# Key products of chunks 24 to 31 made four to fifteen steps earlier, from compact inputs, and copied out by ScalarE

## The chip, the cores and the metric

One core of a Trainium2 chip. The metric is the device time of one execution in microseconds. Three runs of the kernel before gave 883.72, 884.16 and 885.75 us; the median, 884.16 us, is what the changed kernel is compared with.

## The reference

Three layers follow each other. The first, linear attention with a delta rule, is the one that the change touches. With 4 batches, 8 heads, 768 tokens and heads of 48 numbers it does, for each head, token by token:

```python
k_n = k / (np.linalg.norm(k, axis=-1, keepdims=True) + 1e-06)
for t in range(S):
    y[:, :, t] = np.einsum('bhd,bhde->bhe', q[:, :, t], state)
    v_old = np.einsum('bhde,bhd->bhe', state, kt)
    state = state + bt[:, :, :, None] * np.einsum('bhd,bhe->bhde', kt, vt - v_old)
```

The second layer adds the real part of a 2D Fourier transform to its input, normalises and applies a two-layer network (384 to 1536 to 384). The third is a gated network with a 768 by 768 matrix over the tokens. Both come after attention and are not touched.

## The kernel before

**Chunks and steps.** Attention is worked in chunks of 64 tokens: 4 batches of 12 chunks, 48 chunks in all, of 8 heads each (4 pairs of heads, two heads side by side on the partitions). The batches are staggered by four chunks, and the list `SEQ` gives the order. A loop over steps `t` from -3 to 47 (line 516) is a software pipeline: in step t chunk t is finished, and later chunks are prepared. What is recorded in one step stands ahead of what is recorded in the next on each engine (`chain`, line 75), and each engine works through its own list in order.

**What is done for a chunk.** `stage_a` (line 211) multiplies the chunk's keys with its queries and keys on TensorE into a PSUM bank of the tag X (4 banks) and copies the products, masked, into a buffer `gak` that holds four chunks. `solve` (line 267) takes eight chunks at a time, a block: on VectorE it inverts 32 x 32 triangles in some 200 small operations; the class `Spread` deals them out over eight steps, and the block after it is collected by `prep` (line 248) near the end of the same solve. `merge` joins the triangles (TensorE L378 and L380, ScalarE L382 and L385, `diag` L366). `values` scales the values by the norms (ScalarE L402, or VectorE L399 late in the loop). `stage_b` (TensorE L409, ScalarE L414) makes `WU`, `stage_c` (TensorE L425, VectorE L426) makes `cw`, and `stage_d` (TensorE L438 and L440, ScalarE L451 and L455) writes the output and the next state. The order of a step is values, mask, part of the solve, stage_d of chunk t, stage_c of t+1, part of the solve, stage_a, merge and stage_b of t+2, the rest of the step's share of the solve.

**Two ways to make the key products.** Chunks 0 to 7 are made by their own code ahead of the loop. For chunks 8 up to `HEAD` (24 before) `stage_a` reads a compact input `kc` (two chunks per 448 KB transfer), makes eight matmuls of 48 rows (L219) and has ScalarE copy the bank out in three operations (L194, L195, L225), with no mask but for one quarter. What the copy leaves out is made good later: by `mask_q` on VectorE (one operation of 512 columns, L241, or two of 256, L245) in the even step two before the chunk is used, and by five memsets on GpSimd in `root` (L145). All sixteen chunks of this kind are made ahead of the loop, while VectorE solves block 0. From chunk `HEAD` on `stage_a` reads `kq` (one chunk per 448 KB), makes four matmuls of 112 rows (L221) and has VectorE mask and copy in a single operation (L227). These are made in step t for chunk t + 20 (`R`), so chunks 24 to 31 in steps 4 to 11. `prep` of block 3 waits, in the recording, until chunk 31 has been made (line 321).

**Buffers and queues.** `gak` buffers of chunks 0 to 11, 24 to 35 come from the pool `pe`, three of them, the others from another pool. The key inputs have five buffers, refilled by `load_kq` through SyncE's queue: up to step 1 the loop starts the loads of chunks `HEAD` to `HEAD` + 4, and `stage_a` starts the rest.

Of the kernel before, what the change touches and what calls it, by code (L numbers as in the profile page):

```python
# [7 lines left out]
F32 = mybir.dt.float32  # L8
# [14 lines left out]
HP = H // 2  # L23
# [4 lines left out]
GA = C + 2 * D  # L28
NT = B * S // 128

HEAD = 24

TOK = np.concatenate([np.arange(S // 2), [S // 2], S - np.arange(1, S // 2)])

# [31 lines left out]
class Kernel:  # L66
# [51 lines left out]
    def attention(self, cp, pg, pe, p, x, filler, after_solves):  # L118
# [17 lines left out]
        def root(blk):  # L136

            Tf, T, Tw, sq = preps[blk]
            n0 = pe.tile([128, 32], F32, name="n0", bufs=2)
            nc.scalar.sqrt(n0, sq)  # L140
            if blk in (1, 2):

                for n in (16, 8, 4, 2, 1):
                    t = Tw[:, n : n + 1056].rearrange("p (m q) -> p m q", q=66 * n)[:, :, : 32 * n]
                    nc.gpsimd.memset(t.rearrange("p m (r w) -> p m r w", w=32)[:, :, :, :n], 0.0)  # L145
            preps[blk] = Tf, T, sq, n0
# [22 lines left out]

        def ring(bc):  # L170

            gak = (pe if bc // 4 % 6 < 3 else p).tile([128, 4, HP, GA], F32, name="gak", bufs=3)
            for i in range(4):
                gas[bc + i] = gak[:, i]
            gas[bc, 4] = gak
# [16 lines left out]
        def copy_g(out, in_):  # L192

            nc.scalar.activation(out[:, :, 32:], in_[:, :, 32:], AF.Copy, scale=mk[:, 4 * C : 4 * C + 1])  # L194
            nc.scalar.copy(out=out[:, :, :32], in_=in_[:, :, :32])  # L195

        def mask_a(bc, n):
            m = 2 * C if SEQ[bc][1] < HALF else 0
            return mk[:, m : m + n].unsqueeze(1)

        def load_kq(bc):
            if bc < HEAD:
                if 8 <= bc and bc % 2 == 0:
                    t = pe.tile([112, HP, 4 * C], F32, name="kq", bufs=CF["kq"]).rearrange("p a n -> p (a n)")
                    kqs[bc], kqs[bc + 1] = (t[:, i * HP * 2 * C : (i + 1) * HP * 2 * C].rearrange("p (a n) -> p a n", a=HP) for i in range(2))
                    load(out=t.rearrange("p (c n) -> p c n", c=2), in_=a["kc"][:, bc - 8 : bc - 6])
            elif bc < NBC:
                kqs[bc] = pe.tile([112, HP, 4 * C], F32, name="kq", bufs=CF["kq"])
                load(out=kqs[bc], in_=a["kq"][bc])

        def stage_a(bc):
            kq = kqs.pop(bc)
            if bc % 4 == 0:
                ring(bc)
            pa = self.bank("pa", [128, HP, 2 * C])
            for hp in range(HP):
                if bc < HEAD:
                    for r, q in ROWS:
                        nc.tensor.matmul(pa[q, hp], lhsT=kq[r, hp, C:], rhs=kq[r, hp], start=True, stop=True)  # L219
                else:  # L220
                    nc.tensor.matmul(pa[:, hp], lhsT=kq[:, hp, 2 * C :], rhs=kq[:, hp, : 2 * C], start=True, stop=True)  # L221
            if bc < HEAD:

                copy_g(gas[bc][:, :, C : 2 * C], pa[:, :, C:])
                nc.scalar.copy(out=gas[bc][:, :, :C], in_=pa[:, :, :C])  # L225
            else:
                nc.vector.tensor_tensor(  # L227
                    out=gas[bc][:, :, : 2 * C], in0=pa, in1=mask_a(bc, 2 * C).to_broadcast([128, HP, 2 * C]), op=MUL
                )
            if bc < HEAD:  # L230
                if bc % 2 and bc + 2 * CF["kq"] < HEAD:
                    load_kq(bc + 2 * CF["kq"] - 1)
            else:
                load_kq(bc + CF["kq"])
            seen_a[0] = bc + 1
# [152 lines left out]
        def load_kv(bc):  # L388
            load(out=gas[bc][:, :, C:], in_=a["kv"][bc])
# [70 lines left out]
        for n in "kq":  # L460
            t = p.tile([128, 4, HP, GA], F32, name="gak", bufs=3).rearrange("p a b c -> p (a b c)")[:112, :2048]
# [38 lines left out]
        Spread(solve(0), 0).finish()  # L500
        for i in range(4):
            nc.scalar.copy(out=both0(i, 0), in_=pairs0("q", i))
        for bc in range(8, HEAD):
            stage_a(bc)
        busy(CF["last"], 512)
        mask_q(0)
# [8 lines left out]
        T0 = -3  # L515
        for t in range(T0, NBC):
            j, i = divmod(t + 11, 8)
            if i == 0 and j < NB:
                if solver:
                    solver.finish()  # L520
                solver = Spread(solve(j), 25100 if j < NB - 1 else 26500)
            part = (lambda f: solver.upto((i + f) / 8)) if j < NB else (lambda f: None)
            if light(t) and solver:
                solver.finish()
                solver = None

            if 0 <= t + 2 < NBC and (not light(t) or (t + 2) % 8 == 0):
                values(t + 2)
            if t % 2 == 0 and 2 <= t + 2 < HEAD:
                mask_q(t + 2)  # L530
            part(c1)
            if t >= 0:
                stage_d(t)
                if SEQ[t][1] == NC - 1:
                    fill.extend(filler(SEQ[t][0]))
            new = t % 8 == 5 and t + 3 < NBC
            if new:

                merge((t + 3) // 2, True, False)
                load_kv(t + 3)  # L540
                load_kv(t + 4)
                diag((t + 3) // 2)
            if 0 <= t + 1 < NBC:
                stage_c(t + 1)
            if light(t + 1) and t + 3 < NBC and (t + 3) % 8:
                values(t + 3)
            part(c2)
            if HEAD <= t + R < NBC:
                stage_a(t + R)
            if t < T0 + CF["kq"]:  # L550
                load_kq(HEAD + t - T0)
            odd = t % 2 and (t + 3) // 2 < NBC // 2
            if t == NBC - 12:
                solver.finish()
                loads, tail = after_solves()
            if t % 2 == 0 and t % 8 != 4 and t + 4 < NBC:
                diag((t + 4) // 2)
            if (odd or light(t + 1)) and 0 <= t + 2 < NBC:
                stage_b(t + 2)
            if odd:  # L560
                g = (t + 3) // 2
                merge(g + 1, (g + 1) % 4 > 0, True)
                if (t + 5) % 8 and t + 5 < NBC:
                    load_kv(t + 5)
                    load_kv(t + 6)
            if light(t + 1):

                for _ in range(CF["dfs"][t - (NBC - 12)]):
                    while fill and next(fill[0], 1) == 1:
                        fill.pop(0)  # L570
                for _ in range(CF["cvt"][t - (NBC - 12)]):
                    next(tail, None)
            elif not odd and 0 <= t + 2 < NBC:
                stage_b(t + 2)
            if 2 <= t + 4 < NBC:
                load_qt(t + 4)
            part(1)
            self.chain()
            next(loads, None)
            self.chain()  # L580
# [647 lines left out]
```

## Time and profile before

| what | value |
|---|---|
| three runs | 883.72, 884.16, 885.75 us |
| the profiled execution: its own time | 881.6 us |
| span of its instructions | 879.8 us |
| mean granted TensorE clock | 0.986 of full speed |
| TensorE busy | 845.1 us, 7219 instructions |
| VectorE busy | 577.6 us, 1790 instructions |
| ScalarE busy | 392.8 us, 970 instructions |
| GpSimd busy | 72.5 us, 85 instructions |

The attention loop runs from 42 us to 290 us of the span; the two networks fill the rest. In the rows PE is TensorE, PEld its weight load, DVE VectorE, ACT ScalarE, POOL GpSimd and SP SyncE. Each fp32 matmul of the kernel leaves two records (384 records of L438 for 192 matmuls), and records of matmuls overlap, so that a stretch in which TensorE is 100% busy can hold small stalls. The median of the three runs lies 2.56 us above the profiled execution's own time.

### The profile page before, as it was taken

Reading aid. Unit: us, or ns where it says so; the run is one execution under the profiler, and the core shown is the slowest. Engines: PE = TensorE matmul, PEld = TensorE weight load, DVE = VectorE, ACT = ScalarE, POOL = GpSimd, SP = SyncE. Lnnn points to the kernel's source line nnn. Section 1 sums busy time; section 2 is a strip of 40 time slices with the busy share of each in tenths; the row PEclk is TensorE's granted clock in tenths of the full one; section 3 lists DMA queues with packets and bytes.
Section 4 is the critical chain, followed back from the end, with each engine's and each line's share of the span. In section 5 each row is a group of like instructions: output and inputs, shape, how many; then the busy total and the mean of one; then the engine's idle time right before and its main releaser. Section 6 shows DMA issues by size and latency. Waiting matters only on the chain.

```text
span 879.8 us, 18531 instructions
## 1 busy us (share of the span) xinstructions
PE 845.1 (96%) x7219; PEld 816.1 (93%) x7219; DVE 577.6 (66%) x1790; ACT 392.8 (45%) x970; POOL 72.5 (8%) x85
## 2 busy tenths in 40 slices
PE   7879999999998999999999999999999999999998
PEld 7769989998987898999999999999899899899998
DVE  5999999998868897784654993331566552552622
ACT  1569888888765534222122342221352341431511
POOL 2000000000000000000000000000123232231321
PEclk8969999999999999999999999999999999999999
DMA  8265665523461800001022410101122210000001
GB/s 219 66 185 138 169 183 159 158 83 103 127 178 38 322 1 2 1 1 28 1 70 76 129 28 24 48 7 45 58 74 69 71 28 28 27 1 28 28 1 54
DMA packets 57673, 67.21 MB, mean 76 GB/s; under 512 B 31825, under 2 KB 48946, under 8 KB 57586
## 3 DMA queue, kind: packets, MB, share of 16 engines
q1 hardware_dynamic: 57586, 66.03, 26.0%
q8 instruction: 57, 0.93, 0.4%
q14 instruction: 30, 0.25, 0.1%
HBM read 53.62 MB, written 4.72 MB: 66 GB/s over the span
## 4 chain that ended last, share of the span: by engine, by line
PE 78%; DVE 16%; DMA 2%; ACT 2%; issue 1%; POOL 0%; ACTq 0%; SPq 0%; DVEq 0%; POOLq 0%
PE bankX L812 15%; PE bankY L828 14%; PE bankX L951 11%; PE bankY L971 6%; PE bankX L937 5%; PE bankX L912 5%; PE bankY L438 3%; PE bankY L440 3%; PE bankY L425 3%; PE bankY L409 3%; PE bankX L221 2%; DVE tm L308 2%; DVE Ts L313 2%; PE bankX L631 2%; PE bankZ L380 2%; PE bankV L828 1%
## 5 line engine op out<-in xcount | busy, mean ns | idle before, releaser
L812 PE MATMUL bankX<-uh,w 128*128 128x384 f32 x504 | 136.1, 337 | 0.7 <-DVE ul L740 0.7
L828 PE MATMUL bankY<-w,hh 128*128 128x384 f32 x504 | 117.1, 338 | 1.2 <-DVE w L714 1.2
L820 DVE SCALAR_TENSOR_TENSOR hl<-bankX,hh 128x384 fp32r<-128x384 f32 x84 | 46.5, 553 | 97.8 <-ACT hh L819 97.8
L819 ACT ACTIVATE hh<-bankX 128x384 fp32r<-128x384 f32 x84 | 41.2, 491 | 153.7 <-PE bankX L812 150.9
L951 PE MATMUL bankX<-ws,vh 128*128 128x384 f32 x384 | 97.6, 336 | 0.0
L812 PEld LDWEIGHTS bankX<-uh,w 128*128 128x128 f32 x504 | 91.6, 188 | 1.2 <-DVE ul L740 0.9
L828 PEld LDWEIGHTS bankY<-w,hh 128*128 128x128 f32 x504 | 89.9, 188 | 2.3 <-DVE w L714 2.0
L812 PE MATMUL bankX<-ul,w 128*128 128x384 f32 x252 | 84.5, 335 | 0.0
L929 POOL TENSOR_TENSOR vl<-v,vh 128x512 fp32r<-128x512 f32 x24 | 31.8, 1334 | 510.4 <-DMA x<-un 433.9
L438 PE MATMUL bankY<-WU,gak 128*112 128x96 f32 (+1 forms) x384 | 69.6, 269 | 2.7 <-ACT x L455 2.7
L828 PE MATMUL bankY<-w,hl 128*128 128x384 f32 x252 | 71.9, 336 | 0.0
L951 PEld LDWEIGHTS bankX<-ws,vh 128*128 128x128 f32 x384 | 69.4, 188 | 0.0
L440 PE MATMUL bankY<-Sb,cw 112*112 112x96 f32 (+1 forms) x352 | 63.8, 263 | 5.5 <-DVE cw L426 4.6
L959 DVE TENSOR_TENSOR g<-bankX,bsb 128x384 f32<-128x384 f32 x32 | 17.7, 556 | 77.9 <-PE bankX L951 72.0
L951 PE MATMUL bankX<-ws,vl 128*128 128x384 f32 x192 | 63.7, 336 | 0.0
L313 DVE TENSOR_TENSOR Ts<-Ts,tm 128x110 f32<-128x110 f32 (+26 forms) x264 | 59.8, 266 | 0.9
L308 DVE TENSOR_TENSOR tm<-Ts 128x110 f32<-128x110 f32 (+26 forms) x264 | 59.4, 265 | 0.4
L438 PEld LDWEIGHTS bankY<-WU,gak 128*112 128x112 f32 (+1 forms) x384 | 51.7, 176 | 6.0 <-ACT x L455 3.4
L409 PE MATMUL bankY<-gak,TT 128*128 128x96 f32 x384 | 52.2, 281 | 3.9 <-ACT gak L402 3.5
L440 PEld LDWEIGHTS bankY<-Sb,cw 112*112 112x112 f32 (+1 forms) x352 | 47.7, 174 | 7.2 <-DVE cw L426 5.7
L414 ACT COPY WU<-bankY 64x384 f32<-64x384 f32 x96 | 45.4, 473 | 18.8 <-PE bankY L409 17.4
L409 PEld LDWEIGHTS bankY<-gak,TT 128*128 128x128 f32 x384 | 48.8, 199 | 4.5 <-ACT gak L402 4.0
(181 smaller groups left out, 1825.9 us busy)
## 6 DMA issues: line engine op xcount, KB each, us to landing
kq<-in_kq_dram SPq DMA_DIRECT2D x24, 448.0 KB, 4.2
qt<-in_qt_dram SPq DMA_DIRECT2D x48, 196.0 KB, 3.7
gak<-in_kv_dram SPq DMA_DIRECT2D x48, 192.0 KB, 3.8
w<-in_w_dram SPq DMA_DIRECT2D x24, 384.0 KB, 7.7
x<-un SPq DMA_DIRECT2D x128, 36.0 KB, 1.9
out_dram<-ot SPq DMA_DIRECT2D x24, 192.0 KB, 2.0
kq<-in_kc_dram SPq DMA_DIRECT2D x8, 448.0 KB, 11.8
s<-in_wi_dram SPq DMA_DIRECT2D x6, 512.0 KB, 4.3
```

What stands on the lines that cost most here:

```text
L308: nc.vector.tensor_tensor(out=tm, in0=T[:, r, k : k + 1].to_broadcast(sh), in1=T[:, k : k + 1, :k].to_broadcast(sh), op=MUL)
L313: nc.vector.tensor_add(o, o, tm)
L409: nc.tensor.matmul(pb[:, hp].rearrange("p t d -> p (t d)"), lhsT=tt[:, o + hp], rhs=kv[:, hp], start=True, stop=True)
L414: nc.scalar.copy(out=o_, in_=pb[hs])
L438: nc.tensor.matmul(pd[:m, hp], lhsT=ak[:, hp, :m], rhs=u[:, hp], start=True, stop=(c == 0))
L440: nc.tensor.matmul(pd[:m, hp], lhsT=cw[:, hp, :m], rhs=sb[:, hp], start=False, stop=True)
L812: nc.tensor.matmul(ph, lhsT=w1[f][i][:, c * 128 : c * 128 + 128], rhs=cur[k][:, c], start=(c + j == 0), stop=(c == 2 and j == 2))
L820: nc.vector.scalar_tensor_tensor(out=hl, in0=ph, scalar=0.0, in1=hh.bitcast(F32), op0=MAX, op1=SUB)
L828: nc.tensor.matmul(acc[t], lhsT=hx[i][:, t * 128 : t * 128 + 128], rhs=w2[e][k], start=(e == 0 and j == 0), stop=(e == 11 and j == 2),)
L912: nc.tensor.matmul(pv, lhsT=xT[t // 3][i][:, c, (t % 3) * 128 : (t % 3) * 128 + 128], rhs=wi[2 * c + 1][k], start=(c + j == 0), stop=(c == ...
L951: nc.tensor.matmul(pv, lhsT=vn[i][:, s, f * 128 : f * 128 + 128], rhs=ws[2 * s + hf][k], start=(s + j == 0), stop=(s == 5 and j == 2),)
L971: nc.tensor.matmul(po, lhsT=gt[i][:, f, t * 128 : t * 128 + 128], rhs=wo[f][k], start=(f + j == 0), stop=(f == 3 and j == 2),)
```

## The change

`HEAD` goes from 24 to 32, so that chunks 24 to 31 are of the compact kind too: they are read from `kc`, made by the eight small matmuls, copied by ScalarE, masked by `mask_q` on VectorE in steps 22 to 28 and by GpSimd in `root` of block 3. They are not made ahead of the loop with the sixteen others but in steps -3, -2, -1 and 0, two in each. No key products are made in steps 4 to 11; from step 12 on everything stands as before. The pool `pe` holds five `gak` buffers in place of three.

```diff
-HEAD = 24
+HEAD = 32
...
-            if blk in (1, 2):
+            if 0 < 8 * blk < HEAD:
...
-            gak = (pe if bc // 4 % 6 < 3 else p).tile([128, 4, HP, GA], F32, name="gak", bufs=3)
+            gak = (pe if bc // 4 % 6 < 3 else p).tile([128, 4, HP, GA], F32, name="gak", bufs=5 if bc // 4 % 6 < 3 else 3)
...
-        for bc in range(8, HEAD):
+        for bc in range(8, HEAD - 8):
             stage_a(bc)
...
             part(c2)
+            if t < T0 + 4:
+                for i in range(2):
+                    stage_a(HEAD - 8 + 2 * (t - T0) + i)
             if HEAD <= t + R < NBC:
                 stage_a(t + R)
```

On ScalarE, at the start of step -2, the list of before reads as follows; `ZS` and `TT` belong to the merge, `gak` in L402 is the values, `WU` the copy of stage_b, and the numbers tell the buffers apart.

```order
L382 ACTIVATE ZS_80<-bankZ 96x8x32
L366 COPY TT_85<-Tc 32x8x32 x2
L382 ACTIVATE ZS_81<-bankZ 96x8x32
L385 COPY TT_85<-bankZ 32x8x64 x2
L402 ACTIVATE gak<-gak,n_all 128x48 x4
L366 COPY TT_86<-Tc 32x8x32 x2
L414 COPY WU_87<-bankY 64x4x2x48 x2
```

In the changed kernel the stretch from the same L366 to the first L402 stands so:

```order
L366 COPY TT_85<-Tc 32x8x32 x2
L194 ACTIVATE gak<-bankX,mk 128x4x32
L195 COPY gak<-bankX 128x4x32
L225 COPY gak<-bankX 128x4x64
L194 ACTIVATE gak<-bankX,mk 128x4x32
L195 COPY gak<-bankX 128x4x32
L225 COPY gak<-bankX 128x4x64
L382 ACTIVATE ZS_81<-bankZ 96x8x32
L385 COPY TT_85<-bankZ 32x8x64 x2
L402 ACTIVATE gak<-gak,n_all 128x48 x4
```

Six copies, those of chunks 24 and 25, have come between the merge's copies; six more stand in each of steps -2, -1 and 0, behind L402, behind L402 and behind L455.

On VectorE, at the end of the solve of block 2 (steps 11 and 12), the list of before reads as follows; L254 and L261 are `prep` of block 3, L327 turns the finished triangles of block 2.

```order
L426 TENSOR_TENSOR cw<-qt,bankY 112x448
L227 TENSOR_TENSOR gak<-bankX,mk 128x4x128
L254 SCALAR_TENSOR_TENSOR Cc<-gak,mk 128x512 x2
L261 STREAM_TRANSPOSE Ts<-Cc 128x1024
L263 COPY sq<-Ts 128x32
L245 TENSOR_TENSOR gak<-gak,mk 128x4x64 x2
L327 STREAM_TRANSPOSE Tc<-Ts 128x16x32 x2
```

In the changed kernel the same place reads:

```order
L254 SCALAR_TENSOR_TENSOR Cc<-gak,mk 128x512 x2
L261 STREAM_TRANSPOSE Ts<-Cc 128x1024
L263 COPY sq<-Ts 128x32
L426 TENSOR_TENSOR cw<-qt,bankY 112x448
L245 TENSOR_TENSOR gak<-gak,mk 128x4x64 x2
L327 STREAM_TRANSPOSE Tc<-Ts 128x16x32 x2
```

The L227 of chunk 31 is gone, and the collecting of block 3 now stands ahead of step 11's `cw` and no longer behind it.

On TensorE, in step 4, before:

```order
L440 MATMUL bankY<-Sb_89,cw 112x96
L221 MATMUL bankX<-kq 128x128 x4
L409 MATMUL bankY<-gak,TT_86 128x96 x4
L438 MATMUL bankY<-WU_88,gak 112x96 x4
L378 MATMUL bankZ<-Tc,gak 32x32 x16
```

And in the changed kernel:

```order
L440 MATMUL bankY<-Sb_89,cw 112x96
L409 MATMUL bankY<-gak,TT_86 128x96 x4
L438 MATMUL bankY<-WU_88,gak 112x96 x4
L378 MATMUL bankZ<-Tc,gak 32x32 x16
L425 MATMUL bankY<-gak,WU_87 112x112 x4
```

The four matmuls of the key products have left step 4, and likewise steps 5 to 11; sixteen of L219 stand in each of steps -3 to 0.

## Rows read from the trace of the kernel before

**Rows 1.** Windows at steps: length; PE, PEld, DVE, ACT, POOL busy; clock; DMA share, GB/s
```profile
42.00:57.76 15.76, 8.37 (x176) 7.44 (x176) 15.11 (x69) 7.55 (x21) 0.83 (x6) 0.58 0.57 152
57.76:75.18 17.42, 16.94 (x218) 16.24 (x217) 16.97 (x69) 16.55 (x46) 0.00 (x0) 0.89 0.56 157
75.18:114.31 39.13, 38.61 (x572) 37.15 (x568) 37.30 (x152) 33.97 (x95) 0.83 (x6) 1.00 0.59 164
...
193.97:230.35 36.38, 33.62 (x524) 31.64 (x520) 33.00 (x94) 30.35 (x78) 0.15 (x1) 1.00 0.32 84
```

**Rows 2.** Chain of waits, 75.18 to 114.31: by line; a piece (start, us)
```profile
by line: PE bankX L221 18.6%; PE bankY L409 17.7%; PE bankY L438 16.9%; PE bankY L425 15.4%; PE bankY L440 15.2%; PE bankZ L380 8.4%; DVE Ts L261 5.1%; PE bankZ L378 3.5%; PE bankY L444 1.9%; DVE cw L426 1.6%; issue 0.3%; DVE sq L263 0.1%
...
77.75 0.92 PE bankX L221 x8
```

**Rows 3.** Groups by line, 76 to 114 us: count, busy us, mean ns, idle before
```profile
L227 DVE TENSOR_TENSOR gak<-bankX,mk 128x512 f32<-128x512 f32 x8 | 5.5, 691 | 0.4 <-PE bankX L221 0.3
```

**Rows 4.** Timeline of ScalarE, steps -3 to -1: start, us, operation, [idle before]
```profile
45.93 0.23 ACT L140 ACTIVATE n<-sq 128x32 f32<-128x32 f32 x1 [8.13 <-DVE sq L263]
...
48.49 0.38 ACT L382 ACTIVATE ZS<-bankZ 96x256 f32<-96x256 f32 x1 [1.21 <-PE bankZ L380]
...
52.58 0.96 ACT L414 COPY WU<-bankY 64x384 f32<-64x384 f32 x2 [0.65 <-PE bankY L409]
...
56.06 0.96 ACT L414 COPY WU<-bankY 64x384 f32<-64x384 f32 x2 [1.49 <-PE bankY L409]
57.98 0.38 ACT L382 ACTIVATE ZS<-bankZ 96x256 f32<-96x256 f32 x1 [0.95 <-PE bankZ L380]
58.37 1.17 ACT L385 COPY TT<-bankZ 32x512 f32<-32x512 f32 x2
```

**Rows 5.** Timeline of ScalarE ahead of the loop: the three copies of one chunk
```profile
36.13 0.37 ACT L194 ACTIVATE gak<-bankX,mk 128x128 f32<-128x128 f32 x1
36.40 0.26 ACT L195 COPY gak<-bankX 128x128 f32<-128x128 f32 x1
36.54 0.39 ACT L225 COPY gak<-bankX 128x256 f32<-128x256 f32 x1
```

**Rows 6.** Windows of L219 alone: PE and PEld busy us (records), clock, DMA
```profile
21.44:23.14 1.70, 1.70 (x16) 1.70 (x18) 0.50 0.00 0
28.02:29.72 1.70, 1.70 (x36) 1.70 (x34) 1.00 0.84 241
```

**Rows 7.** Windows of steps -3 to 1, four us each, as in rows 1
```profile
42.00:46.00 4.00, 0.61 (x32) 0.49 (x32) 3.83 (x5) 0.07 (x1) 0.04 (x1) 0.83 0.56 126
...
54.00:58.00 4.00, 4.00 (x73) 3.66 (x74) 4.00 (x24) 1.54 (x6) 0.00 (x0) 0.50 0.29 78
...
62.00:66.00 4.00, 4.00 (x75) 3.91 (x76) 4.00 (x21) 3.83 (x12) 0.00 (x0) 1.00 0.68 221
```

**Rows 8.** Timeline of VectorE, steps 11 and 12
```profile
112.54 0.69 DVE L227 TENSOR_TENSOR gak<-bankX,mk 128x512 f32<-128x512 f32 x1 [0.28 <-PE bankX L221]
113.15 1.40 DVE L254 SCALAR_TENSOR_TENSOR Cc<-gak,mk 128x512 f32<-128x512 f32 x2
...
116.69 0.76 DVE L245 TENSOR_TENSOR gak<-gak,mk 128x256 f32<-128x256 f32 x2
```

**Rows 9.** Timeline of TensorE: L409 in step -2, the stalls of steps 4 and 13
```profile
50.47 2.02 PE L409 MATMUL bankY<-gak,TT 128*128 128x96 f32 x8 [2.05 <-ACT gak L402]
...
76.14 0.44 PE L440 MATMUL bankY<-Sb,cw 112*112 112x96 f32 x2 [0.52 <-DVE cw L426]
...
119.93 0.43 PE L440 MATMUL bankY<-Sb,cw 112*112 112x96 f32 x2 [1.03 <-DVE cw L426]
```

**Rows 10.** Timeline of VectorE, a mask in step 0, and steps 27 and 28
```profile
58.51 0.69 DVE L241 TENSOR_TENSOR gak<-gak,mk 128x512 f32<-128x512 f32 x1
...
191.30 0.62 DVE L426 TENSOR_TENSOR cw<-qt,bankY 112x448 f32<-112x448 f32 x1 [1.40 <-PE bankY L425]
```

**Rows 11.** Windows around the start of the loop: DMA in the last columns
```profile
36.00:42.00 6.00, 4.68 (x31) 2.25 (x29) 5.93 (x25) 1.65 (x7) 0.00 (x0) 1.00 0.00 0
```

## What the change was predicted to do

> **What bounds the kernel now.** I read three views in this order. First the windows, cut where a step's first matmul of stage_d starts [rows 1]. The third row is the stretch that the change empties, steps 4 to 11: 39.13 us, in which TensorE is busy 38.61 us, VectorE 37.30 and ScalarE 33.97. So two engines are full there and the third nearly. The row above it, steps 0 to 3, already has no key products on TensorE or VectorE; it takes 17.42 us with 16.94, 16.97 and 16.55 us busy, all three full. The first row, steps -3 to -1, is VectorE's: 15.11 of 15.76 us, while TensorE is busy for 8.37 and ScalarE for 7.55. Second the chain of waits of steps 4 to 11 [rows 2]: nearly all of it is TensorE, and the key products, L221, are its largest line with 18.6%. So what leaves TensorE there leaves the path, until the next engine is late. Third the timeline of ScalarE in steps -3 to -1 [rows 4], because it gets the work: its idle time between 47 and 58 us stands in four waits of 1.21, 0.65, 1.49 and 0.95 us, 4.30 us in all. The wait of 8.13 us before them can't be used: the operation that waits is queued ahead of all that is added.
>
> **What leaves steps 4 to 11.** Eight times four matmuls of L221 at 0.92 us [rows 2] are 7.4 us of TensorE, and eight L227 on VectorE [rows 3] at 0.61 us from start to start (112.54 to 113.15 [rows 8]; their durations of 0.69 overlap) are 4.9 us. That would leave 38.61 - 7.4 = 31.2 us on TensorE, 37.30 - 4.9 = 32.4 on VectorE and an unchanged 33.97 on ScalarE [rows 1]. ScalarE becomes the fullest engine, and 33.97 us is the floor of these steps: at best 5.2 us are won, not 7.4. An engine doesn't reach its floor when it hands work back and forth with two others. The nearest rows that show how close it comes are steps 0 to 3, with the same work by kind and ScalarE full: 17.42 / 4 = 4.36 us a step, 34.8 us for eight; the one extra of steps 4 to 11 is L444, 1.9% of the chain or 0.7 us [rows 2], of which I take 0.5. That gives 35.3 us, a gain of 3.8. The other end is steps 28 to 35, which also make no key products and take 36.38 us with each engine busy for under 34 [rows 1]: a gain of 2.75. I take 3.8, as the work of steps 0 to 3 is the nearer (in steps 28 to 35 part of the scaling of the values stands on VectorE), and keep 2.75 and 5.2 as ends.
>
> **What steps -3 to 0 get.** Per chunk TensorE gets sixteen records of L219 and ScalarE three copies. The copies start 0.27 and 0.14 us apart and the last takes 0.39 [rows 5], so a chunk costs 0.80 us by its end, less the some 0.1 us by which an operation overlaps the one behind it; I take 0.75 (ends 0.70 and 1.02, the sum of the durations). Six chunks in steps -3 to -1 are 4.5 us against 4.30 us of idle time [rows 4]: ScalarE leaves these steps 0.2 us late. The waits can be filled only if what they wait for comes in time. Their releasers are TensorE's merge and L409, behind which the new matmuls are queued. At the full clock two chunks take 2 x 16 / 36 x 1.70 = 1.5 to 1.75 us [rows 6] and stand in TensorE's idle time (7.4 of 15.76 us), so they cost nothing; the cover goes if the clock is low, which is the first rival. Step 0 gives two more chunks, 1.5 us, to a ScalarE that has no idle time left: 1.7 us late. Behind these copies are queued diag, then L414 of chunk 2, on which TensorE's L425 and then VectorE's `cw` wait, so the delay reaches all three engines. Steps 1 to 3 have 17.42 - 16.55 = 0.87 us of idle ScalarE time, of which I let it win back 0.5. Step 4 starts 1.2 us late. Ends: 0, if VectorE alone set the pace of these steps, and 4.6, the first rival's.
>
> **Masks, prep and loads.** `mask_q` for chunks 24 to 31 adds two pairs of L245 (0.76 us each [rows 8]) and two L241 (0.69 [rows 10]) to VectorE in steps 22, 24, 26 and 28, 2.9 us. Up to step 26 VectorE has them done before step 27, where it sits idle for 1.40 us [rows 10] and so is not the last; the fourth stands behind that wait, between the collecting of block 5 and the turning of block 4, where VectorE is late, and costs its 0.6. I take 0.6; ends 0 and 2.9. The collecting of block 3 no longer waits for chunk 31: before, it starts at 113.15, behind chunk 31's L227, and step 13 then stalls TensorE for 1.03 us, where step 4, in which the same collecting stands ahead of `cw`, stalls it for 0.52 [rows 9]. I take a gain of 0.5; ends 0 and 1.0. The five memsets on GpSimd stand a step ahead of their first reader and cost nothing. Loads: four more compact transfers, 1.8 MB, go out before the loop where the DMA engines move nothing for 6 us [rows 11], which at 241 GB/s [rows 6] is 7.5 us, some of it before 36 us; eight of 448 KB leave steps 4 to 11. SyncE's queue has passed them before the loop's first loads, which stand behind them. No cost. Chunks 32 on find buffers free earlier than before, with five in place of three.
>
> **Sum.** +1.2 (start), -3.8 (steps 4 to 11), -0.5 (step 13), +0.6 (masks) = -2.5 us. Nothing behind step 28 is changed in order, and the networks start when attention ends, so it is carried to the end. The profiled execution took 881.6 us (1.8 of it around the span), so its like takes 879.1; it lies 2.56 under the median of the runs, 884.16, and from that the forecast is 881.7 us. The ends add up to -6.2 (0 - 5.2 - 1.0 + 0) and +4.8 (4.6 - 2.75 - 0 + 2.9).
>
> **Rival one, slower: TensorE stays at half its clock.** The granted clock fell to 0.5 of full speed (1.2 GHz of 2.4) when TensorE had done 0.61 us of work in 4 us, stayed there through 54 to 58 us although TensorE was busy then, and was full again in 62 to 66 [rows 7]. At half the clock sixteen records of L219 take 1.70 us [rows 6], two chunks 3.4. TensorE's merge of step -3 ends at 48.4, when L382 can start [rows 4]; then chunks 26 and 27 go until 51.8, L409, 2.02 us at this clock [rows 9], until 53.8, chunks 28 and 29 until 57.2, L409 until 59.2, the merge (1.9, from L414's start at 56.06 to L382's at 57.98) until 61.1, and L382 and L385 (1.55) until 62.7. In rows 4 that last copy ends at 58.37 + 1.17 = 59.54: 3.1 late, 4.6 with step 0's copies. If steps 4 to 11 then run at the pace of steps 28 to 35, the sum is 4.6 - 2.75 + 0.6 = +2.5, 886.6 us. It decides from a delay of some 3.7 us on at step 4: there the gain of the other terms is used up. For it: 54 to 58. Against: the added matmuls close the gaps in which the clock fell. The Trainium skill, "TensorE: Matmul & The Clock Gate", section "Why this matters for your kernels", says that continuous matmuls bring the clock to full and idle gaps lose it; by that rule this rival falls and the time is the forecast's, 881.7. The trace agrees for the fall, with 0.61 us of work in 4, and for the rise behind 58 us; it does not say whether small matmuls like L219 are enough.
>
> **Rival two, no change.** Steps 4 to 11 come only to the pace of steps 28 to 35 (-2.75), ScalarE wins nothing back (+1.7), and two of the four masks are on the path (+1.4): with -0.5 for step 13 it is -0.15, 884.0 us. For it: three engines at 31 to 34 us of work in a ring of waits; against: steps 0 to 3.
>
> **Rival three, a larger gain.** VectorE alone sets the pace up to step 3, so that step 4 starts on time, and ScalarE comes to its floor: -5.2 - 0.5 + 0.6 = -5.1, 879.1 us. For it: VectorE is busy for 4.00 of 4 us in 54 to 58 and in 62 to 66 [rows 7]; against: ScalarE's 16.55 of 17.42 us.
>
> **How the numbers follow.** Two runs differ by about 0.2%, 1.8 us, without meaning anything. Chances: forecast 0.48, rival one 0.16, two 0.28, three 0.08. The forecast's own range is 880.4 to 882.8; some of it, 0.03, lies within 0.2%. Faster: 0.45 + 0.08 = 0.53. Rival one gives 0.13 to slower (over 885.9) and 0.03 to the middle, rival two 0.02 to slower. Same: 0.32; slower: 0.15. The range of 8 in 10 leaves out half of rival three below and half of rival one above: 879.4 to 886.2.
>
> **What would show it.** Right: the windows between the same matmuls of stage_d give some 35 us for steps 4 to 11 with ScalarE the fullest; step 4 starts about 1 us later; the four waits of rows 4 are gone; step 13's stall is about half. Wrong: 39 us again in steps 4 to 11 with waits for L414 or `cw` would mean that the ring of waits and not an engine's work set the pace; a clock of 0.5 at 54 us and step 4 more than 3 us late would be rival one; a gain over 5 us would mean that ScalarE was never close to a bound.

## The result, and the profile after

The changed kernel takes 888.18 us (median of 17 runs, 884.90 to 892.12), the kernel before 884.06 (17 runs beside them, 880.74 to 886.52). The ratio, estimated from all these runs, is 1.0056 with a 95% interval of 1.0043 to 1.0069 (the quotient of the medians, 1.0047, lies in it): about half a per cent slower, where 881.7 us and a gain had been forecast. The profiled execution took 887.73 us (span 885.9, mean granted clock 0.979) against 881.6 before. The chunks are made seven steps earlier (chunk 24, from step 4 to -3) to eleven (chunk 31, from 11 to 0); the "four to fifteen" of the title is wrong.

The stretches that answer to [rows 1], of the changed kernel: steps -3 to -1, 0 to 3, 4 to 11, then 22 to 29 and 40 to 46. Columns as there: length; TensorE, its weight load, VectorE, ScalarE, GpSimd busy; granted clock; DMA share and GB/s.

```profile
41.42:60.43 19.01, 17.66 (x259) 15.88 (x253) 17.81 (x81) 12.09 (x39) 0.83 (x6) 0.54 0.45 127
60.43:79.76 19.33, 18.73 (x251) 17.58 (x249) 14.48 (x57) 18.16 (x52) 0.00 (x0) 0.93 0.52 142
79.76:114.88 35.12, 33.01 (x508) 30.39 (x505) 33.71 (x143) 33.70 (x95) 0.82 (x6) 1.00 0.35 93
166.04:205.46 39.42, 36.73 (x548) 35.01 (x545) 37.35 (x149) 32.73 (x90) 0.15 (x1) 1.00 0.38 103
247.71:293.38 45.67, 40.78 (x409) 38.36 (x406) 29.07 (x71) 25.87 (x62) 0.00 (x0) 0.89 0.32 92
```

The last two of the kernel before, which stand in none of its rows above:

```profile
166.17:204.28 38.11, 36.43 (x548) 34.94 (x545) 34.81 (x142) 32.73 (x90) 0.15 (x1) 1.00 0.37 103
246.55:287.39 40.84, 36.15 (x409) 33.57 (x406) 28.90 (x71) 25.71 (x62) 0.00 (x0) 1.00 0.36 102
```

To compare the start, a mark is needed that the change doesn't move: the first L254 behind the solve of block 0 (42.33 us before, 41.42 after). Step 0 starts 15.44 us behind it before and 19.01 after, step 4 32.85 and 38.34. So between the two profiled executions the start costs +5.49 us, steps 4 to 11 give -4.01 (39.13 to 35.12), steps 12 to 21 -0.70 (51.86 to 51.16), steps 22 to 29 cost +1.31: +2.1 in all. The rest of the difference is the mark itself (-0.91) and steps 40 to 46 (+4.83), in which nothing was changed; they are taken up below.

The loss at the start shows first in TensorE's clock. Four us each from 46 us on, in steps -3 to 0, changed kernel [rows 7]:

```profile
46.00:50.00 4.00, 4.00 (x80) 3.83 (x70) 3.78 (x20) 3.93 (x13) 0.16 (x1) 0.50 0.52 135
50.00:54.00 4.00, 4.00 (x30) 3.50 (x28) 4.00 (x28) 3.57 (x12) 0.00 (x0) 0.50 0.96 289
54.00:58.00 4.00, 4.00 (x32) 3.67 (x29) 4.00 (x20) 2.73 (x11) 0.00 (x0) 0.50 0.02 7
58.00:62.00 4.00, 4.00 (x75) 3.66 (x75) 1.88 (x10) 2.28 (x5) 0.00 (x0) 0.50 0.20 48
```

TensorE is busy all the time and has half its clock all the time; the record of the clock says 0.5 from 42.79 to 63.27 us. The chain of waits of the same stretch, 45 to 62 us (by line, and four of its pieces with start and length), is TensorE almost alone:

```profile
by line: PE bankX L219 42.5%; PE bankY L409 23.0%; PE bankZ L380 14.8%; PE bankY L438 9.1%; PE bankZ L378 7.5%; ACT ZS L382 1.6%; ACT n L140 1.3%; DVE sq L263 1.2%; issue 0.4%
...
47.52 3.61 PE bankX L219 x32
51.13 1.95 PE bankY L409 x8
53.08 3.61 PE bankX L219 x32
56.69 1.95 PE bankY L409 x8
```

The new matmuls are the largest line. The half clock itself is not new: in the kernel before it lasts 17.07 us (44.65 to 61.71) against 20.48 now. But VectorE set the pace there [rows 1]; now VectorE waits, 1.88 us of work in the last of the four windows. On ScalarE the four waits of [rows 4] are not gone but have moved: copies of the added chunks (L194 and the two behind it) stand among them, and ScalarE still waits for TensorE.

```profile
53.17 0.96 ACT L414 COPY WU<-bankY 64x384 f32<-64x384 f32 x2 [0.37 <-PE bankY L409]
...
56.73 0.37 ACT L194 ACTIVATE gak<-bankX,mk 128x128 f32<-128x128 f32 x1 [0.75 <-PE bankX L219]
...
58.73 0.96 ACT L414 COPY WU<-bankY 64x384 f32<-64x384 f32 x2 [1.20 <-PE bankY L409]
60.64 0.38 ACT L382 ACTIVATE ZS<-bankZ 96x256 f32<-96x256 f32 x1 [0.95 <-PE bankZ L380]
```

That L382 starts 2.66 us later than in [rows 4] (57.98), and 3.57 later against the mark.

In steps 4 to 11 the change does what was forecast. The chain of waits there, in which L221 had 18.6% [rows 2], now has ScalarE's L402, L385, L451 and L455 among its lines (the row is as the view gives it, cut at its end):

```profile
by line: PE bankY L438 15.4%; PE bankY L409 12.6%; PE bankY L440 11.9%; PE bankY L425 11.6%; ACT gak L402 8.3%; PE bankZ L380 7.3%; ACT TT L385 5.2%; ACT Sb L451 5.1%; ACT x L455 4.1%; issue 3.5%; PE bankZ L378 3.3%; ACT ZS L382 3.0%; ACT W
```

And VectorE at the end of block 2 collects block 3 ahead of step 11's `cw` [rows 8]; the stall of 1.03 us in step 13 [rows 9] is gone, and step 13 takes 5.27 us in place of 6.54. Step 12 takes 4.81 in place of 4.22, so that steps 12 to 21 give 0.70 us and not 1.27.

```profile
111.46 1.41 DVE L254 SCALAR_TENSOR_TENSOR Cc<-gak,mk 128x512 f32<-128x512 f32 x2
112.90 1.96 DVE L261 STREAM_TRANSPOSE Ts<-Cc 128x1024 f32<-128x1024 f32 x1
115.00 0.61 DVE L426 TENSOR_TENSOR cw<-qt,bankY 112x448 f32<-112x448 f32 x1
115.53 0.75 DVE L245 TENSOR_TENSOR gak<-gak,mk 128x256 f32<-128x256 f32 x2
```

The masks of steps 22 to 28 are dearer than forecast. VectorE's wait of 1.40 us ahead of step 27's `cw` [rows 10] has shrunk to 0.18, so they do fill it, but steps 25 and 27 are still 0.37 and 0.28 us longer. And the last of them, at 197.21, makes TensorE wait 1.52 us in step 29, where it waited 0.91 before (VectorE, then TensorE):

```profile
191.88 0.62 DVE L426 TENSOR_TENSOR cw<-qt,bankY 112x448 f32<-112x448 f32 x1 [0.18 <-PE bankY L425]
...
197.21 0.68 DVE L241 TENSOR_TENSOR gak<-gak,mk 128x512 f32<-128x512 f32 x1
```
```profile
200.44 0.41 PE L440 MATMUL bankY<-Sb,cw 112*112 112x96 f32 x2 [1.52 <-DVE w L152]
```

### The profile page after: what moved, and what is told of

Same layout as the page of the kernel before. It is cut to its first block, busy times and chain, and to the rows that moved or that the text cites. A ratio compares the mean times of both kernels' runs of the same rounds, so it can differ in the third digit from the quotient of the medians.

```text
span 885.9 us, 18679 instructions
## 1 busy us (share of the span) xinstructions
PE 854.7 (96%) x7283; PEld 823.0 (93%) x7283; DVE 575.5 (65%) x1788; ACT 398.3 (45%) x994; POOL 73.2 (8%) x90
## 4 chain that ended last, share of the span: by engine, by line
PE 76%; DVE 17%; ACT 3%; DMA 2%; issue 1%; SPq 0%; POOL 0%; ACTq 0%; DVEq 0%; POOLq 0%
PE bankX L815 15%; PE bankY L831 14%; PE bankX L954 11%; PE bankY L974 6%; PE bankX L940 5%; PE bankX L915 5%; PE bankY L438 3%; PE bankY L440 3%; PE bankY L425 3%; DVE tm L308 2%; DVE Ts L313 2%; PE bankY L409 2%; PE bankX L634 2%; PE bankV L831 1%; PE bankZ L380 1%; DVE cw L426 1%
## 5 line engine op out<-in xcount | busy, mean ns | idle before, releaser
L438 PE MATMUL bankY<-WU,gak 128*112 128x96 f32 (+1 forms) x384 | 71.6, 275 | 4.0 <-ACT x L455 3.9
L440 PE MATMUL bankY<-Sb,cw 112*112 112x96 f32 (+1 forms) x352 | 65.6, 269 | 4.9 <-DVE cw L426 3.2
L438 PEld LDWEIGHTS bankY<-WU,gak 128*112 128x112 f32 (+1 forms) x384 | 53.5, 182 | 7.7 <-ACT x L455 5.2
L414 ACT COPY WU<-bankY 64x384 f32<-64x384 f32 x96 | 45.4, 473 | 16.4 <-PE bankY L409 14.9
L409 PE MATMUL bankY<-gak,TT 128*128 128x96 f32 x384 | 52.1, 280 | 0.5 <-DVE gak L399 0.4
L940 PE MATMUL bankX<-xh,s 128*128 128x384 f32 x192 | 50.3, 338 | 1.0 <-ACT v L924 1.0
```

The costliest lines, as they stand in the source:

```text
L409: nc.tensor.matmul(pb[:, hp].rearrange("p t d -> p (t d)"), lhsT=tt[:, o + hp], rhs=kv[:, hp], start=True, stop=True)
L414: nc.scalar.copy(out=o_, in_=pb[hs])
L438: nc.tensor.matmul(pd[:m, hp], lhsT=ak[:, hp, :m], rhs=u[:, hp], start=True, stop=(c == 0))
L440: nc.tensor.matmul(pd[:m, hp], lhsT=cw[:, hp, :m], rhs=sb[:, hp], start=False, stop=True)
L940: nc.tensor.matmul(pu, lhsT=wi[2 * c][i][:, f * 128 : f * 128 + 128], rhs=xT[hf][k][:, c], start=(c + j == 0), stop=(c == 2 and j == 2),)
```

## The experiments

All times below are of the profiled execution of each kernel, the start as step 4's distance from the mark; where the clock is the same, a stretch comes back to within 0.2 us from kernel to kernel (0.4 in steps 4 to 11 of the old order).

| kernel | step 4 | steps 4-11 | 12-21 | 22-29 | 30-39 | 40-46 | ratio to before, 95% |
|---|---|---|---|---|---|---|---|
| before | +32.85 | 39.13 | 51.86 | 38.11 | 42.27 | 40.84 | |
| before again | +32.83 | 38.88 | 53.20 | 38.08 | 42.26 | 42.34 | 0.9993, 0.9980 to 1.0006 |
| changed | +38.34 | 35.12 | 51.16 | 39.42 | 42.26 | 45.67 | 1.0056, 1.0043 to 1.0069 |
| 1 fill | +35.24 | 35.11 | 51.13 | 39.40 | 42.23 | 44.95 | 1.0016, 1.0001 to 1.0030 |
| 2 ahead | +35.30 | 35.10 | 51.16 | 43.52 | 43.24 | 44.23 | 1.0001, 0.9988 to 1.0015 |
| 3 full size | +34.46 | 35.11 | 51.13 | 42.72 | 41.69 | 43.34 | 1.0023, 1.0005 to 1.0040 |
| 4 GpSimd | +38.49 | 35.10 | 51.17 | 43.57 | 42.24 | 43.82 | 1.0061, 1.0038 to 1.0085 |
| 5 ahead, fill, GpSimd | +33.56 | 35.12 | 51.13 | 40.41 | 42.26 | 43.73 | 0.9997, 0.9982 to 1.0012 |
| 6 six chunks | +34.86 | 35.11 | 51.15 | 42.51 | 41.43 | 43.93 | 1.0005, 0.9993 to 1.0016 |
| 7 before, fill | +33.69 | 38.74 | 51.84 | 38.08 | 42.26 | 45.17 | 0.9979, 0.9965 to 0.9994 |
| 8 ahead, fill | +33.41 | 35.10 | 51.20 | 42.16 | 43.22 | 43.69 | 1.0007, 0.9991 to 1.0022 |
| 9 as 8, masks early | +33.30 | 35.13 | 51.16 | 38.11 | 42.27 | 45.39 | 0.9966, 0.9950 to 0.9982 |
| 10 before, fill as 8 | +33.89 | 38.77 | 51.85 | 38.11 | 42.27 | 44.11 | 1.0005, 0.9989 to 1.0020 |
| 11 changed, masks early | +38.20 | 35.11 | 51.19 | 38.09 | 42.26 | 45.49 | 1.0021, 1.0009 to 1.0033 |

**1. The clock kept full by dummy matmuls.** Eight more matmuls of 512 columns, whose result nobody reads (eight ahead of the loop in place of four, and two in each of steps -2 and -1):

```diff
-        busy(CF["last"], 512)
+        busy(8, 512)
...
+            if t in (T0 + 1, T0 + 2):
+                busy(2, 512)
```

> The changed kernel with more dummy matmuls: eight in place of four behind the last chunk made ahead of the loop, and two of 512 columns behind the key products of steps -2 and -1 each, so that TensorE has no idle gap around 42 us and few until 56 us. Theory A (the half clock of 42.8 to 63.3 us makes the late start): the granted clock is full through steps -2 to 0, step 4 starts by 77.5 us in place of 79.8, and the time falls by 2 to 4 us against the changed kernel. Rival B (the 24 ScalarE copies make the late start whatever the clock is): step 4 starts at 79 us or later and the time stays within 1 us of the changed kernel's.

The clock is full from 22 to 251 us, and step 4 comes at +35.24: with the half clock 3.10 of the 5.49 us are gone, as theory A had it, and 2.39 remain. The two windows (-3 to -1, 0 to 3) and, in step 1, what the late `cw` waits for (TensorE, ScalarE, VectorE):

```profile
41.52:58.01 16.49, 15.25 (x283) 11.27 (x283) 15.84 (x72) 11.82 (x39) 0.83 (x6) 1.00 0.57 146
58.01:76.76 18.75, 17.38 (x251) 16.25 (x248) 16.34 (x68) 17.98 (x53) 0.00 (x0) 1.00 0.56 146
```
```profile
65.25 1.04 PE L425 MATMUL bankY<-gak,WU 128*112 128x112 f32 x8 [0.89 <-ACT WU L414]
```
```profile
64.23 0.97 ACT L414 COPY WU<-bankY 64x384 f32<-64x384 f32 x2
```
```profile
66.33 0.62 DVE L426 TENSOR_TENSOR cw<-qt,bankY 112x448 f32<-112x448 f32 x1 [2.15 <-PE bankY L425]
```

ScalarE works without a pause from 58.22 to 65.20, six copies of step 0 and diag among it, before L414 of chunk 2 is done; TensorE and then VectorE wait for it. The 2.39 split into 1.05 before step 0 (16.49 - 15.44) and 1.34 in steps 0 to 3 (18.75 - 17.41). How much of the 1.05 is the dummies' own, experiment 7 bounds.

**2. All eight chunks ahead of the loop**, none in steps -3 to 0:

```diff
-        for bc in range(8, HEAD - 8):
+        for bc in range(8, HEAD):
...
-            if t < T0 + 4:
-                for i in range(2):
-                    stage_a(HEAD - 8 + 2 * (t - T0) + i)
```

> The changed kernel with chunks 24 to 31 made ahead of the loop, with the sixteen others, and none in steps -3 to 0. Theory A (clock and queue in steps -3 to 0 are the loss, and steps 4 to 11 really win some 4 us): step 4 starts within 1.5 us of the kernel before's 75.2 us, steps 4 to 11 take 35 to 36 us, and the time is 1 to 4 us below the kernel before. Rival C (steps 4 to 11 were short only because they began late, with work piled up): they take 37 us or more and the time is that of the kernel before.

Steps 4 to 11 take 35.10 us, which rules out rival C. But step 4 is 2.45 us late all the same, for a new reason. TensorE has the dummies of L491, which in the kernel before ended 1.73 us ahead of the mark, only now, behind the added L219, and the merge stands behind them; ScalarE waits for the merge (TensorE, then ScalarE). The clock is also at half here, from 50.91 to 64.56 us; what of the 2.45 us is its part is not separated. The rows:

```profile
43.49 3.70 PE L491 MATMUL bankY<-TT 128*128 128x512 f32 x8
```
```profile
47.87 0.38 ACT L382 ACTIVATE ZS<-bankZ 96x256 f32<-96x256 f32 x1 [1.88 <-PE bankZ L378]
```

**3. Matmuls of full size in steps -3 to 0.** The products of chunks 24 to 31 come from the full inputs by L221 (four of 112 rows a chunk), but are still copied by ScalarE (the loads of the inputs are moved to suit, not shown):

```diff
-                if bc < HEAD:
+                if bc < 24:
                     for r, q in ROWS:
...
-            if bc < HEAD:
+            if bc < 24:
                 if bc % 2 and ...
```

> The changed kernel with chunks 24 to 31 still made in steps -3 to 0 and copied out by ScalarE, but from the full inputs with four matmuls of 112 rows by 128 columns each in place of eight of 48 by 64. Theory A2 (the small matmuls do not bring the clock back): the clock is full again by 57 us in place of 63.3, and step 4 starts 1.5 us or more ahead of the changed kernel's 79.8. Rival (any matmul counts alike, the clock's return depends on something else): half clock until 60 us or later, step 4 at 79 us or later.

The clock is at half from 43.30 to 53.54 us, 10.24 us. In the three profiles of the changed kernel's own order (changed, 4 and 11) it is so for 20.48, 20.48 and 17.07 us, although in this kernel and in the changed one TensorE has no idle time from 46 us until its clock is full again (here the rows of kernel 3):

```profile
50.00:54.00 4.00, 4.00 (x22) 4.00 (x22) 4.00 (x28) 3.79 (x13) 0.00 (x0) 0.56 0.81 199
54.00:58.00 4.00, 4.00 (x93) 3.81 (x92) 4.00 (x20) 3.90 (x15) 0.00 (x0) 1.00 0.94 253
```

That points to the kind of the added matmuls (48 rows by 64 columns against 112 by 128) and not to gaps between them. It rests on one profile of this kernel, but the runs agree: the median of their mean granted clocks is 0.984 (10 runs) against 0.978 (17 runs of the changed kernel). Step 0 is on time (+15.36); step 4 is 1.6 us late, all of it from steps 0 to 3.

**Before again.** The kernel before, unchanged, to see by what two profiles of one kernel differ.

> The kernel before once more, for the granted clock of several executions. If the half-clock stretches of steps 40 to 47 in the changed kernel's profile (three of 3.4 us) are the change's doing, the mean clock is 0.986 in every execution here. If they come by chance to both kernels, the mean clock varies between 0.976 and 0.986 and the time with it by some 5 us.

Its start is the same to 0.02 us; its steps 12 to 21 and 40 to 46 each have one stretch at half clock and are 1.3 and 1.5 us longer than in the profile that the prediction was made from. The mean clocks of its ten runs lie between 0.978 and 0.983, so that the profile of before, with 0.986, was a fast one by luck.

**4. The masks of chunks 24 to 31 on GpSimd**, in the changed kernel:

```diff
-                nc.vector.tensor_tensor(out=out, in0=out, in1=m, op=MUL)
+                (nc.gpsimd if bc >= 24 else nc.vector).tensor_tensor(out=out, in0=out, in1=m, op=MUL)
```

> The changed kernel with the four masks of chunks 24 to 31 on GpSimd, which stands idle there, in place of VectorE. Theory (the masks cost VectorE time in steps 22 to 28, 1.3 us in the span of steps 22 to 29, and their idle time on TensorE in step 29 makes a half-clock stretch there more likely): steps 22 to 29 fall from 39.42 to about 38.1 us as in the kernel before, the rest stays, so 886.7 us at 885 of the kernel before. Rival (the 1.3 us come from somewhere else, for instance from GpSimd's memsets of block 3 or the later buffers): steps 22 to 29 stay at 39.4 us. Second rival (GpSimd shares a path to the buffers with VectorE or is so slow that stage_d waits for it): steps 22 to 29 over 39.4 us.

Steps 25, 27 and 29 are back at 4.48, 5.61 and 6.30 us, as before the change (4.48, 5.59, 6.36): that the masks were the cause is shown. But step 23 takes 10.87 us in place of 5.34. GpSimd does all masks at once, when its queue comes to them in step 21 (GpSimd, then VectorE, then VectorE of the changed kernel at the same place):

```profile
163.56 2.79 POOL L245 TENSOR_TENSOR gak<-gak,mk 128x256 f32<-128x256 f32 x4
166.30 2.50 POOL L241 TENSOR_TENSOR gak<-gak,mk 128x512 f32<-128x512 f32 x2
```
```profile
164.36 1.37 DVE L286 SCALAR_TENSOR_TENSOR Ts<-Ts 128x30 f32<-128x30 f32 x2
165.65 0.68 DVE L227 TENSOR_TENSOR gak<-bankX,mk 128x512 f32<-128x512 f32 x1
166.25 2.98 DVE L286 SCALAR_TENSOR_TENSOR Ts<-Ts 128x29 f32<-128x29 f32 x4
```
```profile
163.89 0.59 DVE L286 SCALAR_TENSOR_TENSOR Ts<-Ts 128x30 f32<-128x30 f32 x2
164.39 0.68 DVE L227 TENSOR_TENSOR gak<-bankX,mk 128x512 f32<-128x512 f32 x1
164.99 0.81 DVE L286 SCALAR_TENSOR_TENSOR Ts<-Ts 128x29 f32<-128x29 f32 x4
```

L286, which reads two operands in SBUF, takes 4.35 us (1.37 + 2.98) in place of 1.40 (0.59 + 0.81), 2.95 us more; L227, which reads one of its two in PSUM, takes its 0.68 as ever. The Trainium skill, "SBUF — State Buffer", section "SBUF: two separate sides", says that the two engines share one pair of ports, held by one operation whole: an operation of VectorE with two SBUF inputs and one of GpSimd that reads SBUF shut each other out. The rows agree with that. TensorE then waits 2.19 us for the `cw` of step 23, and in this execution a half-clock stretch follows (173.19 to 180.01).

**5. As 2, with GpSimd's masks, no dummies ahead of the merge and two in each of steps -2 and -1:**

```diff
-        busy(CF["last"], 512)
...
+            if t in (T0 + 1, T0 + 2):
+                busy(2, 512)
```

> All eight chunks ahead of the loop, without the four dummy matmuls ahead of the first merge, two dummy matmuls of 512 columns in each of steps -2 and -1, and the masks of chunks 24 to 31 on GpSimd. Theory (the start was held up by the dummies ahead of the merge, 3.6 us, and by the clock; the masks cost 1.3 us): step 4 at +32.8 to +33.6 us from the loop's mark as before, steps 4 to 11 in 35.1, step 12 at +68 to +68.7, steps 22 to 29 in 38.1: 880 to 881 us against 884.5 of the kernel before, ratio about 0.996. Rival (the sixteen matmuls L219 and the copies ahead of the loop hold up the start by themselves): step 4 at +35 as in the run with the dummies, 883 us, ratio 0.998 to 0.999.

The start is within 0.7 us of the kernel before, as the theory said, and the time is not better, since step 23 stands still for 2.2 us as in 4.

**6. Six chunks in steps -3 to -1, none in step 0, the dummies of 1:**

```diff
-        for bc in range(8, HEAD - 8):
+        for bc in range(8, HEAD - 6):
...
-            if t < T0 + 4:
+            if t < T0 + 3:
                 for i in range(2):
-                    stage_a(HEAD - 8 + 2 * (t - T0) + i)
+                    stage_a(HEAD - 6 + 2 * (t - T0) + i)
```

> The changed kernel with chunks 24 and 25 ahead of the loop and the six others in steps -3 to -1, none in step 0, eight dummy matmuls ahead of the loop and two in each of steps -2 and -1 (which in an earlier run kept the clock full). Theory (at full clock the 2.4 us that step 4 is late come from ScalarE's queue in step 0, whose six copies stand ahead of stage_b's of chunk 2): step 4 at +33 to +33.8 us from the loop's mark in place of +35.24. Rival (the copies of all four steps delay alike, or the L219 matmuls do on TensorE): step 4 stays at +35 or later.

Half of the theory holds: without step 0's copies steps 0 to 3 take 17.40 us, as in the kernel before, so the 1.34 us of experiment 1 belong to step 0's two chunks. (Their matmuls went with the copies; that it was the copies is read from ScalarE's queue in experiment 1.) But step 0 itself is 2.0 us late, since more L219 and eight dummies stand ahead of the first merge, which starts 3.54 us behind the mark and no longer 0.41 ahead of it. The number came out close to the rival's +35, for another reason.

**7. The kernel before with the dummies of 1.** The same two lines as in 1.

> The kernel before with the same dummy matmuls (eight ahead of the loop in place of four, two in each of steps -2 and -1). Theory (in the kernel before VectorE sets the time of steps -3 to 3, and TensorE's half clock is hidden there): the clock is full in steps -3 to 0 and step 4 still comes at +32.8 +-0.3 us: ratio 0.999 to 1.001. Rival (the half clock costs the kernel before as well, so that the clock is worth the same to both): step 4 at +30 to +31.5, ratio 0.997 to 0.998.

The two answers do not agree. The ratio says 0.2% faster; the profile, its slowest execution (885.95 us of 880.11 to 885.95), has the start 0.84 us later, with a half clock from 48.75 to 55.58, and nothing shorter by as much. Why the runs are faster stays open; the four fastest (880.11 to 880.71) have mean clocks of 0.990 and 0.991, the other eight 0.985 to 0.988, and the profile is not one of the four. But it bounds experiment 1: with the same dummies and no added chunks step 0 comes at +16.29 and step 4 at +33.69. Against that the eight chunks cost 0.20 us up to step 0 and 1.35 in steps 0 to 3, 1.55 in all (kernel 7 has its half clock there, kernel 1 none, so 1.55 may be too low).

**8 and 9. All eight ahead, no dummies ahead of the merge, two in steps -2 and -1, the masks on VectorE** (8 is 5 with the masks as in the changed kernel), **and the same with the masks early** (9):

```diff
-            if t % 2 == 0 and 2 <= t + 2 < HEAD:
+            if t % 2 == 0 and 2 <= t + 2 < 24:
                 mask_q(t + 2)
+            for bc in {13: (24,), 19: (26, 28), 21: (30,)}.get(t, ()):
+                mask_q(bc)
```

> The run with all eight chunks ahead of the loop, no dummies ahead of the first merge and two in each of steps -2 and -1, but with the masks of chunks 24 to 31 on VectorE as in the changed kernel. Theory (GpSimd's masks stopped VectorE's L286 for about 2.9 us in step 21, which made step 23 late; on VectorE the masks cost 1.3 us): step 4 at +33.6 us from the loop's mark, steps 4 to 11 in 35.1, steps 22 to 29 in 39.4 in place of 40.4: about 883 us against 884.6, ratio 0.998. Rival (the stop in step 23 has another cause than GpSimd): steps 22 to 29 stay at 40.4 or more.

> As the run with the masks on VectorE and nothing of the eight chunks in the loop, but the masks of chunks 24 to 31 stand in steps 13 (24 and 25), 19 (26 to 29) and 21 (30 and 31), where TensorE is the fuller engine, and no longer in steps 22 to 28. Theory (the masks cost 1.3 us only because they stand in steps in which VectorE sets the pace): steps 22 to 29 in 38.1 us as before, steps 12 to 21 in 51.1 to 51.5: about 882 us, ratio 0.997. Rival (VectorE's work is one list and a mask costs its 0.75 us wherever it stands): steps 12 to 21 in 52.4 and the ratio no better than 0.998.

Step 23 is back at 5.39 in kernel 8, as the theory said, but steps 22 to 29 take 42.16 and not 39.4: the clock falls to half from 197.98 to 208.22 us, behind the wait of 1.51 us that the last mask makes. With the masks early (9) the wait is 0.93 us, the clock stays, and the added masks cost nothing: steps 13, 19 and 21 take 5.27, 6.27 and 7.01 us, as without them (5.27, 6.28, 6.99 in the changed kernel). In 13 and 19 TensorE is busy throughout; in 21 the mask falls where VectorE used to wait 0.48 us for TensorE. Kernel 8, step 29 (window, TensorE), then kernel 9 in windows of steps -3 to -1, 0 to 3, 4 to 11, 12 to 21 and 22 to 29:

```profile
194.41:204.11 9.70, 8.19 (x130) 7.56 (x129) 6.91 (x24) 5.18 (x14) 0.15 (x1) 0.68 0.26 65
```
```profile
196.35 0.41 PE L440 MATMUL bankY<-Sb,cw 112*112 112x96 f32 x2 [1.51 <-DVE w L152]
```
```profile
41.94:57.83 15.89, 11.99 (x210) 8.27 (x206) 15.24 (x71) 9.50 (x30) 0.83 (x6) 0.79 0.60 150
57.83:75.23 17.40, 15.84 (x219) 14.66 (x216) 16.93 (x69) 16.64 (x47) 0.00 (x0) 1.00 0.58 158
75.23:110.36 35.13, 33.01 (x508) 30.41 (x504) 33.71 (x144) 33.70 (x95) 0.83 (x6) 1.00 0.35 93
110.36:161.53 51.17, 49.52 (x749) 47.15 (x745) 50.07 (x181) 42.61 (x118) 0.98 (x7) 1.00 0.58 158
161.53:199.64 38.11, 36.42 (x547) 34.93 (x544) 34.94 (x143) 32.72 (x90) 0.15 (x1) 1.00 0.40 108
```

Kernel 9 takes 881.70 us (12 runs, 879.25 to 883.63) against 884.28 of the kernel before: ratio 0.9966, 0.9950 to 0.9982. It is faster than the kernel before and the changed one.

**10. The kernel before with the dummies of 8 and 9.** `busy(CF["last"], 512)` goes, `busy(2, 512)` comes in steps -2 and -1.

> The kernel before with the same dummies as those two: none ahead of the first merge, two in each of steps -2 and -1. Theory (VectorE sets the time of steps -3 to 3 of the kernel before, so that neither the dummies ahead of the merge nor the clock matter there): step 4 at +32.8 +-0.4 us, ratio 0.999 to 1.000, and the change is worth 1 to 2 us over this kernel. Rival (the clock is worth as much here, as the ratio of 0.998 with other dummies hints): step 4 at +31 to +32, ratio 0.997 to 0.998, and then the change is worth nothing over the same dummies.

No gain, with the start 1.0 us later than in the kernel before, outside the +-0.4 of the theory. So these dummies alone do not bring kernel 9's gain; with the eight products out of steps 4 to 11 it comes. Over kernel 7, the kernel before with other dummies, a gain is not shown: 0.9966 (0.9950 to 0.9982) and 0.9979 (0.9965 to 0.9994) overlap.

**11. The changed kernel with the masks early**, by the edit of 9 alone.

> The changed kernel, with nothing else touched than the place of the masks of chunks 24 to 31: steps 13, 19, 19 and 21 in place of 22, 24, 26 and 28. Theory (the masks cost the changed kernel 1.3 us in steps 22 to 29, and the longer wait of step 29 often brings a half-clock stretch there that costs 2.8 to 3.7 us more): steps 22 to 29 in 38.1 us, no half clock in step 29, the start as in the changed kernel (step 4 at +38.3): median 2 to 3.5 us below the changed kernel's, ratio to the kernel before 1.001 to 1.003. Rival (the half-clock stretches of step 29 come by chance and were not due to the masks): 1.3 us alone, ratio 1.004 to 1.005.

The ratio falls from 1.0056 to 1.0021 (1.0009 to 1.0033), some 3 us by the ratios and 1.7 by the medians' distances from their kernels before (4.1 and 2.4). Steps 22 to 29 are back at 38.09. Of the six profiles in which the mask of step 28 stands on VectorE, four have a half-clock stretch that begins in step 29 (2, 3, 6, 8; not the changed kernel's own and not 1); of the eight others none has. So the masks cost more than the 1.3 us that the changed kernel's profile shows, in those executions in which the clock falls there. That the longer wait brings the fall is likely by these counts, not certain.

## Why the prediction was wrong

**Steps 4 to 11: right.** 35.3 us forecast, 35.12 measured, and 35.10 to 35.13 in every kernel without the eight products. ScalarE is busy for 33.70 us, near the forecast 33.97, but VectorE, forecast at 32.4, for 33.71, and TensorE for 33.01 in place of 31.2. The chain is still mostly TensorE's (62% by the lines shown), so that ScalarE's work sets a floor there is not shown; what is shown is that the pace of steps 0 to 3 was the right one to carry over, that of steps 28 to 35 not.

**Step 13: the sign right, the size partly by luck.** -0.5 forecast, -0.70 in steps 12 to 21. The stall is gone altogether, not halved, and step 13 gives 1.27 us; step 12, 0.59 longer, which the forecast did not have, takes part of it back.

**The start: the step that failed.** It is the sentence that two chunks' matmuls "stand in TensorE's idle time [...], so they cost nothing; the cover goes if the clock is low". The clock was low, and rival one, given 0.16, is what happened at the start: it put two chunks at 3.4 us (3.61 measured) and step 4 at 4.6 us late (5.49 measured, where the sum had +1.2). The trace of before already had 54 to 58 us at half clock with TensorE busy throughout [rows 7]; that weighed less with me than the argument that the added matmuls close the gaps. The Trainium skill, "TensorE: Matmul & The Clock Gate", section "Why this matters for your kernels", says that continuous matmuls bring the clock to full. The changed kernel does not agree with it from 46 to 62 us; kernel 3, where the matmuls in the same gaps were of full size, does. The clock's part is 3.10 us (changed against 1), up to 3.94 if the 0.84 us of experiment 7 are the dummies' own.

**ScalarE's part of the start: the mechanism right, the size a little low.** Forecast 1.2 us, as 0.2 up to step -1, 1.5 in step 0 and 0.5 won back. With the clock kept full it is 1.55 (1 against 7, the same dummies in both: 0.20 and 1.35), at most 2.39 (1 against before). That the 1.35 are step 0's two chunks, experiment 6 shows. Little was won back in steps 1 to 3.

**Masks: mis-sized.** +0.6 forecast, +1.31 measured. The sentence that up to step 26 the 1.40 us wait hides them was wrong: the wait shrank by 1.22, and 0.65 us came on top. The price of the longer wait of step 29, a half clock in some executions, was not thought of.

**The sum.** -2.5 forecast; by steps it is +2.1 (5.49 - 4.01 - 0.70 + 1.31), and the medians differ by +4.1. Of the 2 us between, the half clock of step 29 explains a part: experiment 11 won 1.7 to 3.1 us, of which 1.3 are the masks' own, so an estimate of that part is 0.4 to 1.8 us. The rest is open. That the 45.67 us of steps 40 to 46 are the change's doing is not shown: these steps vary from 40.84 to 45.17 in kernels of the old order and from 43.34 to 45.67 in the others, for the most part by stretches of half clock, of which the profile of before happened to have none there; that goes with its 2.56 us under the median of its runs. A share of the change in them is not ruled out.

## What to carry to other kernels

Idle time of TensorE is priced at the clock that it has there: look at the granted clock of the stretch into which work is moved, and, as kernel 3 suggests, at the size of the matmuls that go there, before calling the move free. Work that is off the path in one step may be on it in the next, so place it by step (here the same masks cost 1.3 us and, in four of six profiles, a fall of the clock in steps 22 to 28, and nothing in steps 13, 19 and 21). And where a filler stands ahead of something that was early, moving work before the filler makes it late.

## What the runs showed of the hardware

- TensorE busy without a gap from 46 to 62 us, in large part with matmuls of 48 rows and 64 columns (L219), kept half its clock until 63.27 us; with matmuls of 112 rows and 128 columns (L221) in the same places it was full at 53.54 (one profile).
- Tensor operations of GpSimd that read SBUF stretched VectorE's L286 (two SBUF operands) from 0.27 us each to between 0.26 and 1.39, median 0.67, and left L227 and L426 (one operand in PSUM) at 0.68 and 0.62.
- A wait of TensorE of 1.51 us in place of 0.93 in step 29 was followed by a half clock from 197.98 to 208.22 us in one kernel (8) and, at 1.52, by none in another (the changed kernel): the same wait does not always bring it.
